# End-of-kernel semaphore waits split between SyncE and GpSimd, and the last attention tile placed ahead of the last half-row matmuls

## The chip, the cores and the metric

The kernel runs on one core of one Trainium2 chip. The metric is device time in microseconds (us) of one execution. A profile of one execution comes with each kernel; its "span" goes from the first to the last recorded instruction and is about 1.7 us shorter than the device time. All times with two or three decimals are from the trace's records or its views. A semaphore is a counter that an instruction can wait for; the end barrier is the last step of the program, in which the engines wait for each other. TensorE is called PE in profile lines (PEld is its weight load), VectorE DVE, ScalarE ACT, GpSimd POOL, SyncE SP; SPq or POOLq is the sequencer of such an engine, which waits for semaphores and issues transfers.

## The reference, cut to what matters

A gate mixes two branches over the same 2048 tokens of width 640:

```python
g = _sigmoid((x * gate_w).sum(-1, keepdims=True))
a = _A_ref(x, A_wqkv, A_wo)          # linear attention, 32 heads of 20
b = _B_ref(x, B_w1, B_w2, B_w3, B_w4)  # token shifts and an MLP with 1728 hidden units
return g * a + (1 - g) * b
# in _B_ref, the end:
h2 = _gelu(_layernorm(x1, axis=-1) @ w3) @ w4
return x1 + h2
```

For the tiles of 128 tokens the kernel computes an attention tile (`a_tile`), keeps it in a buffer, and adds it to the result of the w4 product (`w4_tile`). The hidden width is 1728, which is 13 blocks of 128 rows and one of 64. The 64-row block of four token tiles is done in one go by `w4_half`: two tiles share TensorE's rows, 64 rows each. These are "the half rows" below; the source's word for the step is an excursion.

## The kernel before: the parts that matter

A small scheduler in the source orders the work items of several streams. An item is released by its dependencies; the streams named "AT" (attention tiles) and "W4" meet here:

```python
for t in range(NT):                       # NT = 16
    ...
    IT.add("AT", ("a", t), 1.33, lambda t=t: a_tile(t), deps)
    deps4 = [(("a", t), 0.0), (("w3h", c - c % 2), GEL), (("w3", c, KFF - 1), GEL)]
    if t % 4 == 0:
        deps4.append((("w3", min(c + 1, NCH - 1), KFF - 1), 0.0))
        if t == 0:
            deps4.append((("a", 3), 0.0))
    elif t + 3 < NT:
        deps4.append((("a", t + 3), 0.0))  # attention runs three tiles ahead
    if t % 4 == 0:
        IT.add("W4", ("w4h", t), 0.76, lambda t=t: w4_half(t), deps=deps4)
    IT.add("W4", ("w4", t), 3.5, lambda t=t: w4_tile(t), deps=deps4)
```

PSUM is the memory that TensorE's results go to; the source divides it into eight banks. `w4_half` takes six of them for four tiles; `w4_tile` adds the 13 full-row blocks into them and VectorE evicts each tile with two `scalar_tensor_tensor` instructions (512 and 128 columns), which add the attention tile and write `x_tok`. For tiles 13 to 15 no later attention tile is demanded, so tile 15's attention (called a(15) below) went where the scheduler found it: between w4 tiles 14 and 15.

At the end of the program SyncE waits for every transfer the kernel ever issued:

```python
for want_out in (False, True):
    for k, n in self.dma_cnt.items():
        if k.startswith("out") == want_out:
            self.prog["sp"].append(([("d:" + k, 16 * n)], None, None))
```

There are 35 keys of inputs, weights and on-chip transposes, and 4 of outputs. The last tile's output leaves in two transfers: 512 columns issued by ScalarE (key out1), 128 columns by SyncE (key out2).

## Time and profile before

| | before |
|---|---|
| device time, median of the first three runs | 262.99 us (262.86 to 263.22) |
| span of the profiled run | 261.28 us |
| TensorE busy | 257.5 us, 99% |
| last matmul starts | 258.47 us |
| last eviction ends | 259.08 us |
| last output lands | 260.735 us |
| end | 261.281 us |

First, some lines of the profile page: span, busy time and share of the span by engine with the number of instructions, granted TensorE clock in 40 slices (tenths), and the chain of work that ended last.

```profile
span 261.3 us, 4300 instructions
PE 257.5 (99%) x1699; PEld 135.7 (52%) x1699; DVE 149.1 (57%) x268; ACT 107.0 (41%) x215; POOL 95.7 (37%) x151
PEclk9999999999999999999999999999999999999999
PE 98%; DVE 1%; issue 0%; POOL 0%; POOLq 0%
```

TensorE is the bottleneck, so only two sorts of time can be won by moving work: holes on TensorE, and the tail after its last matmul.

The timeline around the last group of half rows shows one hole. Columns: start, duration in us, engine, line, operation, what is written from what; in brackets the engine's idle time before it and what ended that.

```profile
241.57 1.08 DVE L647 SCALAR_TENSOR_TENSOR x_tok<-ps,stg,abx 128x512 bf16<-128x512 f32 x2 [1.92 <-PE ps L1106]
242.38 0.10 PEld L1088 LDWEIGHTS ps<-w,h2h 64*128 64x128 bf16 x2 [0.29 <-DVE x_tok L647]
242.38 0.39 PE L1088 MATMUL ps<-w,h2h 64*128 64x512 bf16 x2
```

The half rows of tiles 12 to 15 need the bank that VectorE empties for tile 11, and TensorE waits 0.29 us for it. The chain of waits in order of time (start, duration, what) shows the same: an eviction stands in it between two TensorE stretches.

```profile
20.35 0.81 PE ps L787 x6
...
237.37 1.36 PE ps L608 x10
238.73 2.82 PE ps L1106 x13
...
241.57 0.76 DVE x_tok L647
...
242.38 0.39 PE ps L1088 x2
...
243.10 10.70 PE ps L1106 x78
253.80 1.36 PE ps L608 x10
255.16 2.82 PE ps L1106 x13
257.98 0.03 issue
258.00 1.08 DVE x_tok L647 x2
```

The ten matmuls of 1.36 us at 253.80 are a(15). The first line, the first matmuls of a later stage, will serve as a mark. Its time is always taken from this view, which starts the piece about 0.16 us behind the record of its first matmul (20.191 here).

For the tail, the views of two source lines of before give sequencer instructions (columns: how many, duration in ns as minimum/median/maximum, first and last start). The line of the waits, on SyncE after 259 us:

```profile
L316 SPq EVENT_SEMAPHORE  x19: 28/28/28, 259.5 to 260.8; - x19
```

The line that ends the program:

```profile
L296 SPq COMPARE_BRANCH  x1: 41/41/41, 260.9 to 260.9; - x1
```

And of the list of transfers the last two outputs, with their size and the time from issue to landing:

```profile
out_dram<-x_tok ACTq DMA_DIRECT2D x1, 128.0 KB, 1.8
out_dram<-x_tok SPq DMA_DIRECT2D x1, 32.0 KB, 1.6
```

From 259.5 on SyncE works through 19 wait instructions, each holding two semaphores, and the branch holds the 39th. The first 16 stand 0.062 us apart. It looks as if 1.2 us could be removed. But the last transfer is issued at 259.11 and lands at 260.735, and the end of the program can't come before that.

### The profile page before, as it was taken

How to read it: one execution, taken by the hardware profiler on the slowest of the kernel's cores; microseconds unless marked ns; L12 is line 12 of the kernel's file. 1: busy time of each engine (PE TensorE's matmuls, PEld its weight loads, DVE VectorE, ACT ScalarE, POOL GpSimd, SP SyncE). 2: the span in 40 equal slices, each digit the busy share in tenths (PEclk: the TensorE clock that was granted, in tenths of full speed). 3: DMA queues.
4: the chain of work that ended last, by engine and by line, in shares of the span. 5: the costliest groups of instructions: out<-in, count | busy, mean ns of one | idle time of the engine just before them, and what ended most of it. 6: DMA issues, size and time to landing. Idle time of an engine off the chain costs nothing.

```text
span 261.3 us, 4300 instructions
## 1 busy us (share of the span) xinstructions
PE 257.5 (99%) x1699; PEld 135.7 (52%) x1699; DVE 149.1 (57%) x268; ACT 107.0 (41%) x215; POOL 95.7 (37%) x151
## 2 busy tenths in 40 slices
PE   8999999999999999999999999999999999999996
PEld 4555555555555555554444545554455544455553
DVE  1597887899803799979995407992033410143333
ACT  1496677742365757684874240005500045100000
POOL 5003995859774018687654202320011200011000
PEclk9999999999999999999999999999999999999999
DMA  6855999561567795545666600232000020000311
GB/s 200 253 96 139 187 185 151 173 109 24 79 126 103 213 388 166 76 90 67 108 125 126 103 0 0 47 87 69 0 3 0 3 100 0 3 0 0 103 50 50
DMA packets 50691, 24.82 MB, mean 95 GB/s; under 512 B 42052, under 2 KB 49261, under 8 KB 50672
## 3 DMA queue, kind: packets, MB, share of 16 engines
q1 hardware_dynamic: 49280, 21.15, 36.5%
q0 software_dynamic: 1152, 3.28, 5.9%
q8 instruction: 13, 0.21, 0.3%
q10 hardware_dynamic: 240, 0.13, 0.2%
q14 instruction: 6, 0.05, 0.1%
HBM read 12.05 MB, written 2.62 MB: 56 GB/s over the span
## 4 chain that ended last, share of the span: by engine, by line
PE 98%; DVE 1%; issue 0%; POOL 0%; POOLq 0%
PE ps L608 61%; PE ps L1106 21%; PE ps L787 8%; PE ps L860 2%; PE ps L836 1%; PE ps L1020 1%; PE ps L1088 1%; PE ps L619 1%; DVE x_tok L647 1%; PE ps L861 1%; PE ps L934 1%; PE ps L1085 0%; POOL xn L667 0%; POOLq L1249 0%
## 5 line engine op out<-in xcount | busy, mean ns | idle before, releaser
L608 PE MATMUL ps<-xnT,w 128*128 128x512 bf16 x360 | 82.3, 379 | 0.0
L1106 PE MATMUL ps<-w,h2T 128*128 128x512 bf16 (+1 forms) x416 | 58.8, 299 | 0.0
L664 ACT ACTIVATE h2T<-ps 128x512 bf16<-128x512 f32 x52 | 30.4, 600 | 65.7 <-PE ps L608 65.7
L608 PEld LDWEIGHTS ps<-xnT,w 128*128 128x128 bf16 x360 | 34.0, 98 | 36.9 <-issue 0.4
L647 DVE SCALAR_TENSOR_TENSOR x_tok<-ps,stg,abx 128x512 bf16<-128x512 f32 (+1 forms) x32 | 17.2, 551 | 61.6 <-PE ps L1106 61.6
L630 POOL TENSOR_SCALAR abx<-x_tok,stg 128x640 f32<-128x640 bf16 x16 | 15.4, 962 | 100.7 <-DVE x_tok L647 95.1
L1106 PEld LDWEIGHTS ps<-w,h2T 128*128 128x128 bf16 x416 | 32.4, 98 | 25.6 <-issue 1.1
L630 POOL TENSOR_SCALAR xn<-x_tok,st 128x640 bf16<-128x640 bf16 x32 | 33.6, 1055 | 16.6 <-DMA xnT<-xn 16.1
L664 ACT ACTIVATE Er<-ps 128x640 bf16<-128x640 f32 x32 | 22.6, 705 | 18.0 <-PE ps L608 8.5
L663 ACT ACTIVATE junk<-x_tok 128x640 bf16<-128x640 bf16 x32 | 23.6, 737 | 4.8 <-DVE x_tok L645 4.3
L664 ACT ACTIVATE hsT<-ps 128x512 bf16<-128x512 f32 (+1 forms) x32 | 18.9, 594 | 15.1 <-PE ps L608 14.7
L608 PE MATMUL ps<-M_sb,pqnT 128*128 128x512 bf16 (+1 forms) x160 | 24.3, 299 | 0.0
L787 PE MATMUL ps<-pk_tok,x_tok 128*128 128x512 bf16 (+1 forms) x160 | 23.9, 299 | 0.0
L608 PE MATMUL ps<-w,hsT 128*128 128x512 bf16 (+1 forms) x160 | 23.9, 299 | 0.0
L608 PE MATMUL ps<-wkg,xT 128*128 128x512 bf16 (+1 forms) x150 | 22.6, 299 | 0.0
L647 DVE SCALAR_TENSOR_TENSOR abx<-ps,stg,abx 128x640 f32<-128x640 f32 x16 | 14.2, 884 | 14.7 <-PE ps L608 14.7
L608 PEld LDWEIGHTS ps<-w,hsT 128*128 128x128 bf16 x160 | 13.3, 98 | 12.3
L608 PEld LDWEIGHTS ps<-M_sb,pqnT 128*128 128x128 bf16 x160 | 13.1, 98 | 10.4
L608 PE MATMUL ps<-wq,xT 128*128 128x512 bf16 (+1 forms) x120 | 18.3, 299 | 0.0
L630 DVE TENSOR_SCALAR Er<-Er 128x640 bf16<-128x640 bf16 x32 | 11.8, 369 | 9.5 <-ACT Er L664 9.3
L645 DVE SCALAR_TENSOR_TENSOR x_tok<-ps,x_tok 128x640 bf16<-128x640 f32 x16 | 13.1, 821 | 6.9 <-PE ps L608 6.0
L608 PEld LDWEIGHTS ps<-wkg,xT 128*128 128x128 bf16 x150 | 12.2, 97 | 9.0
(71 smaller groups left out, 232.6 us busy)
## 6 DMA issues: line engine op xcount, KB each, us to landing
w<-in_B_w_dram SPq DMA_DIRECT2D x1, 2160.0 KB, 8.4
w<-in_B_w_dram SPq DMA_DIRECT2D x1, 2080.0 KB, 13.8
x_tok<-in_A_x_dram SPq DMA_DIRECT2D x3, 640.0 KB, 5.8
out_dram<-x_tok SPq DMA_DIRECT2D x3, 640.0 KB, 3.5
w<-in_B_w_dram POOLq DMA_DIRECT2D x8, 160.0 KB, 4.7
wq<-in_A_wqkv_dram SPq DMA_DIRECT2D x5, 160.0 KB, 3.9
wkg<-in_A_wqkv_dram SPq DMA_DIRECT2D x5, 160.0 KB, 4.0
wv<-in_A_wqkv_dram POOLq DMA_DIRECT2D x1, 800.0 KB, 7.1
```

The source lines that it names most:

```text
L608: ins = e.matmul(out_ap, l, r, start=(i == 0), stop=(i == n - 1))
L619: ins = e.transpose(o, s_, ident[:])
L630: return engf(lambda e: e.tensor_scalar(out_ap, in_ap, s1, s2, op0, op1), rd, [out_ap], cost=cost)
L645: return dve(lambda e: e.scalar_tensor_tensor(out_ap, in0, scalar, in1, op0, op1, accum_out=accum), rd, [out_ap, accum], cost=cost + 70.0)
L647: return dve(lambda e: e.scalar_tensor_tensor(out_ap, in0, scalar, in1, op0, op1), rd, [out_ap], cost=cost)
L663: return act(lambda e: e.activation(out_ap, in_ap, func, bias=bias, scale=scale, accum_out=accum), rd, wr, cost=cost)
L664: return act(lambda e: e.activation(out_ap, in_ap, func, bias=bias, scale=scale), rd, wr, cost=cost)
L787: ins = e.matmul(o, l, r, start=(t0 + q_ == 0), stop=(t0 + q_ == NT - 1))
L836: ins = e.matmul(ps[:, b, 0:n], xn[:, 0, 0:128], xn[:, 0, 0:128].unsqueeze(1).to_broadcast([128, n // 128, 128]), start=True, stop=True)
L860: e.matmul(ps[:, b, 0:512], l, w[:, k, 0:512], start=(k == 0), stop=(k == KD - 1))
L861: return e.matmul(ps[:, b + 1, 0:n2], l, w[:, k, 512:512 + n2], start=(k == 0), stop=(k == KD - 1))
L1106: ins = e.matmul(o, l, r, start=False, stop=(i == KFF - 1), skip_group_check=(n0 > 0))
```

## The change

The intent: SyncE shall wait for outputs only, with the last transfer last, while GpSimd, which has finished its work, waits for all else; and a(15) shall stand ahead of the last half rows, where TensorE has a hole. The diff, without its two lines that record the order of the transfers:

```diff
-            for want_out in (False, True):
-                for k, n in self.dma_cnt.items():
-                    if k.startswith("out") == want_out:
-                        self.prog["sp"].append(([("d:" + k, 16 * n)], None, None))
+            last = {}
+            for i, k in enumerate(self.dma_order):
+                last[k] = i
+            for k in sorted(last, key=last.get):
+                self.prog["sp" if k.startswith("out") else "pool"].append(([("d:" + k, 16 * self.dma_cnt[k])], None, None))
@@
             if t == 0:
                 deps4.append((("a", 3), 0.0))
+            if t == NT - 4:
+                deps4.append((("a", NT - 1), 0.0))
```

The source's order is not the program's. The build packs two waits into one instruction, takes them in an order of its own, and leaves the first listed wait on the branch. This is what stands on SyncE behind its last transfer in the two built programs (no profile, only the order):

```
before: 16 instructions with inputs (the last: out0, x23), then (out1, x1), (out2, wq0), (out3, x0), branch waits for touch
after:  (out1), (out2, out0), branch waits for out3
```

Here out1 and out2 carry the last two transfers; all other keys were met long before.

## The prediction

> **What bounds the kernel now.** TensorE. The page's first part gives PE 257.5 us busy of a span of 261.3 (99%), the granted clock is full in all slices, and the chain that ended last is 98% PE. Outside PE there is only the tail: the last matmul starts at 258.47, VectorE ends at 259.08, the output transfers issued at 258.79 (ScalarE, 128 KB) and 259.11 (SyncE, 32 KB) land 1.8 and 1.6 us after issue, at about 260.6 and 260.7, and SyncE's branch, drain and the end barrier take the rest to 261.28.
>
> **Part one: the waits.** SyncE's wait instructions stand 0.06 us apart and hold two semaphores each. Before, 19 of them plus the branch stand after SyncE's last transfer, from 259.50 on. That looks like 1.2 us to remove, but it is hidden: the first 16 are through at 260.45, and the next two start at 260.58 and 260.75, held by the two landings, not by their number. The built program takes the waits of one instruction in another order than the source lists them: before, one more wait (an earlier output with an input) and the branch's own (the first load) stand behind the last landing. After the change SyncE keeps two wait instructions and the branch: the ScalarE output, then the last SyncE output with another, then the branch. So one step of 0.06 us goes; the 1 us of input waits goes from under the landing. GpSimd gets 17 waits; its last work ends near 243.5 and it is idle after, so they cost nothing. Expected: 0.06 us.
>
> **Part two: the attention tile.** The TensorE order differs only here: ten matmuls of the last attention tile (1.36 us in the chain) move from behind the third tile of the last w4 group to in front of that group's half-row matmuls; its addition on VectorE moves with it. In the trace these half-row matmuls wait for VectorE (timeline: weight load at 242.38, idle 0.29 before it, released by the x_tok eviction): matmul starts stand 0.34 us apart instead of 0.056. The moved tile has its operands and its bank long before, and covers the eviction. What stays is the step from full rows to half rows: in the three other groups it costs 0.10 us over the normal pitch (starts 0.31 apart instead of 0.21). The Trainium skill, page "TensorEngine Tiling (Array Packing)", section "Key Properties", says that changing the tiling mode drains TensorE; this trace agrees, with about 0.1 us a change. So 0.28 minus 0.10 = 0.19 us. The half rows now wait also for the tail eviction of the tile before (ends 242.65), well inside the 1.36 us. At the end nothing is added: the removed VectorE wait for an output was met at 256.03; the outputs of tiles 12 to 14 leave about 1.2 us later and land by about 257.3, before the last ones start.
>
> **Sum.** 0.19 + 0.06 = 0.25 us of 263: within 2%, smaller than the spread of the three runs before (0.36). I predict 262.74 us, 262.3 to 263.1.
>
> **What would show it.** Right: span near 261.0; no idle time before the last group's half-row load; the last matmul about 0.19 earlier; 0.06 less from the last landing to the end; SyncE with two waits after its last issue. Wrong: a new wait of TensorE near 242 to 244 (bank, or GpSimd's multiply too late), or a landing over 2 us.
>
> **What could make it wrong.** Another bank order delaying an eviction; GpSimd's waits slow enough to reach the barrier; landing times, which vary by a tenth.

## The result, and the profile after

| | before | after |
|---|---|---|
| device time, median of 6 runs each | 263.06 us (262.56 to 263.22) | 262.88 us (262.41 to 263.14) |
| ratio | | 0.9993, 95% interval 0.998 to 1.0006: the same within 2% |
| span of the profiled run | 261.281 us | 261.218 us |
| start of the mark (first matmuls of L787, later L790) | 20.35 us | 20.54 us |
| mark to the start of the last evictions | 237.65 us | 237.46 us |
| last landing to end | 0.546 us | 0.492 us |

A ratio is the mean time of one kernel's fast runs over that of the other's fast runs of the same rounds, so it is not quite the ratio of the medians. All six runs of each were fast.

The difference of the medians is 0.18 us, less than the scatter of one kernel's runs. The profile can tell what the times cannot. The same views, after:

```profile
span 261.2 us, 4301 instructions
PE 257.6 (99%) x1699; PEld 135.9 (52%) x1699; DVE 149.2 (57%) x268; ACT 106.9 (41%) x215; POOL 95.6 (37%) x151
PEclk9999999999999999999999999999999999999999
PE 98%; DVE 0%; issue 0%; POOL 0%; POOLq 0%
```

The timeline at the half rows:

```profile
241.76 1.08 DVE L650 SCALAR_TENSOR_TENSOR x_tok<-ps,stg,abx 128x512 bf16<-128x512 f32 x2 [1.92 <-PE ps L1109]
242.28 1.52 PE L611 MATMUL ps<-M_sb,pqnT 128*128 128x512 bf16 x10
243.73 0.10 PEld L1091 LDWEIGHTS ps<-w,h2h 64*128 64x128 bf16 x2
243.74 0.39 PE L1091 MATMUL ps<-w,h2h 64*128 64x512 bf16 x2
```

a(15) now runs while VectorE evicts tile 11 (until 242.84), and the half rows have no idle time before them. In the records, the start of the half rows follows the matmul before it by 0.151 us; before it was 0.340.

The chain of waits:

```profile
20.54 0.81 PE ps L790 x6
...
237.56 1.36 PE ps L611 x10
238.91 3.53 PE ps L1109 x26
242.45 1.36 PE ps L611 x10
243.81 0.32 PE ps L1091 x2
...
244.46 13.52 PE ps L1109 x91
257.98 0.02 issue
258.00 1.08 DVE x_tok L650 x2
```

The eviction has left the chain. Yet the last evictions start at 258.00 in both profiles: this run entered the mark 0.19 us later and won 0.19 us in the last group. Had one looked only at the end of the chain, the gain would have been missed.

The tail. First the line of the waits, on SyncE after 259 us and on GpSimd after 242 us:

```profile
L319 SPq EVENT_SEMAPHORE  x2: 17/22/28, 260.6 to 260.7; - x2
L319 POOLq EVENT_SEMAPHORE  x17: 42/43/43, 242.9 to 244.3; - x17
```

Then the line that ends the program:

```profile
L298 POOLq DRAIN  x1: 1942/1942/1942, 244.5 to 244.5; - x1
L298 SPq COMPARE_BRANCH  x1: 41/41/41, 260.8 to 260.8; - x1
```

17 of SyncE's 19 wait instructions are gone, but it now just stands still until the landings at 260.558 and 260.726. The two waits and the branch start at 260.575, 260.742 and 260.815, in place of 260.584, 260.752, 260.814 and 260.879: one step less behind the last landing. GpSimd's 17 waits and the one on its branch are over at 244.4 and its drain at 246.5, over 14 us ahead of the barrier at 261.0.

### The profile page after: what moved, and what is told of

Its sections match the earlier page's. It is cut to its first block, busy times and chain, and to the rows that moved or that the text cites. A ratio compares the mean times of both kernels' runs of the same rounds, so it can differ in the third digit from the quotient of the medians.

```text
span 261.2 us, 4301 instructions
## 1 busy us (share of the span) xinstructions
PE 257.6 (99%) x1699; PEld 135.9 (52%) x1699; DVE 149.2 (57%) x268; ACT 106.9 (41%) x215; POOL 95.6 (37%) x151
## 4 chain that ended last, share of the span: by engine, by line
PE 98%; DVE 0%; issue 0%; POOL 0%; POOLq 0%
PE ps L611 61%; PE ps L1109 22%; PE ps L790 8%; PE ps L863 2%; PE ps L839 1%; PE ps L1023 1%; PE ps L1091 1%; PE ps L622 1%; PE ps L864 1%; PE ps L937 1%; DVE x_tok L650 0%; PE ps L1088 0%; POOL xn L670 0%; POOLq L1254 0%
## 5 line engine op out<-in xcount | busy, mean ns | idle before, releaser
L790 PE MATMUL ps<-pk_tok,x_tok 128*128 128x512 bf16 (+1 forms) x160 | 23.9, 299 | 0.0
```

What stands on the lines that cost most here:

```text
L790: ins = e.matmul(o, l, r, start=(t0 + q_ == 0), stop=(t0 + q_ == NT - 1))
```

## The experiments

The theory has two parts. First, the waits on SyncE lay in the shadow of the last landing, and one step of 0.06 us stood behind it. Second, a(15) covers a hole of 0.28 us in front of the half rows, of which 0.10 us comes back as the cost of changing to half rows. The rivals: each removed wait is time saved (then 1 us was lost elsewhere); the hole is the cost of changing rows and not a wait for a bank; the waits only moved their cost to GpSimd. E1 to E4 ran on one chip, E5 to E8 on another; each had its own runs of the kernel before beside it. E5 to E7: only their traces are used. All results were correct.

### E1: the waits alone

Edit, against the changed kernel:

```diff
-            if t == NT - 4:
-                deps4.append((("a", NT - 1), 0.0))
```

> The waits moved, the attention tile left where it was. My theory (the waits lie under the landing of the last outputs, only one wait instruction of 0.06 us stood behind it): two wait instructions on SyncE after its last issue, 0.49 us from the last landing to the end instead of 0.55, the idle time of about 0.29 us before the half-row weight load near 242.4 still there, time 0.06 us under before. Rival (every removed wait instruction is time saved, 17 of 0.06 us each): the span is about 1.0 us shorter, 260.3, and the time near 262.0.

Measured: median 262.91 us of 6 runs, before 263.26 of 11, ratio 0.9998 (0.9982 to 1.0015); one of its runs was at 264.17 with the full clock, which I can't explain and which lifts the mean. The timeline of E1 at the half rows:

```profile
242.30 0.10 PEld L1091 LDWEIGHTS ps<-w,h2h 64*128 64x128 bf16 x2 [0.29 <-DVE x_tok L650]
```

Its waits on SyncE after 259 us:

```profile
L319 SPq EVENT_SEMAPHORE  x2: 17/22/28, 260.5 to 260.7; - x2
```

From last landing to end it took 0.492 us, from mark to last eviction 237.65, as before. So the hole is untouched, and 17 wait instructions fewer on SyncE won 0.054 us. The rival's span of 260.3 did not come (261.15). The size of 0.06 us rests on the trace; the times can't resolve it.

### E2: the tile alone

Edit, against the kernel before: the two lines that E1 takes out, put in.

> The attention tile moved, the waits left on SyncE. My theory (0.28 us of waiting for VectorE's eviction is covered, 0.10 us of changing from full to half rows stays): no idle time before the half-row load, matmul starts there about 0.15 us apart instead of 0.34, last matmul 0.19 us earlier against the one before the group, 19 wait instructions on SyncE and 0.55 us from last landing to end; time 0.19 us under before. Rival (the 0.34 us are the change of row mode, not the eviction): the starts stay about 0.34 us apart and the time is that of before.

Measured: median 262.84 us of 6 runs, ratio 0.9998 (0.9976 to 1.002), again with one outlier (264.62). The timeline of E2 at the half rows:

```profile
243.70 0.10 PEld L1088 LDWEIGHTS ps<-w,h2h 64*128 64x128 bf16 x2
```

Its waits on SyncE after 259 us:

```profile
L316 SPq EVENT_SEMAPHORE  x19: 28/28/28, 259.5 to 260.8; - x19
```

No idle time before the half rows; their start follows the matmul before by 0.152 us; from mark to last eviction 237.47, 0.18 less than before; from landing to end 0.549, as before. The hole was the wait for the bank. The two parts add up: E1's tail and E2's stretch are those of the changed kernel. The times do not show this: the medians of E1 and E2 lie 0.35 and 0.42 us under before's, more than the traces give (0.05 and 0.18), and each with an outlier. Nothing is read from times at this size.

### E3: last output listed first

Edit, against the changed kernel:

```diff
-            for k in sorted(last, key=last.get):
+            for k in sorted(last, key=last.get, reverse=True):
```

> The changed kernel with its waits listed in the opposite order, last output first, since the built program puts the first listed wait on the branch itself. Theory: the branch then waits for the last landing directly and no wait instruction stands behind it; 0.42 us from last landing to end (0.49 in the changed kernel, 0.55 before); time 0.07 us under the changed kernel. Rival (order plays no part, or the branch costs more when it has to wait itself): 0.49 us or more.

Measured: 0.423 us from last landing to end; the branch starts 0.017 us behind the landing (0.089 in the changed kernel). SyncE's waits are both taken up at 259.5, and the second one stands until ScalarE's output lands:

```profile
L319 SPq EVENT_SEMAPHORE  x2: 17/524/1032, 259.5 to 259.5; - x2
```

The branch of E3, in the view of the line that ends the program:

```profile
L298 SPq COMPARE_BRANCH  x1: 41/41/41, 260.7 to 260.7; - x1
```

Median 262.63 us of 5 runs, ratio to before 0.9981 (0.9969 to 0.9993). By the traces this version beats both kernels, the changed one by 0.07 us and before by 0.31 (0.19 + 0.05 + 0.07); it was not timed beside the changed kernel. The timed gain against before is larger than that sum but its interval holds it. So the intent "last one last" was met in the source and not in the program; listing it first does it.

### E4: three times the input waits on SyncE

Edit, against the kernel before:

```diff
-            for want_out in (False, True):
+            for want_out in (False, False, False, True):
```

> The kernel before, each input wait listed three times: 54 wait instructions on SyncE instead of 19. Theory (the waits are hidden until they reach the landing, with about 0.15 us of room): 259.50 plus 54 steps of 0.062 is 262.85, so the end comes at about 263.3, 2.0 us later than before, and the landing no longer sets the end. Rival one (waits that are already met cost next to nothing, at any number): the time of before. Rival two (each costs in full): 35 times 0.062, 2.2 us later.

Measured: span 263.301; from the mark (20.47) to the end 242.83 us, 1.90 more than before's 240.93 (the other 0.12 us of the longer span are a later start); median 265.20 us of 4 runs, ratio 1.0098 (1.0067 to 1.0129, one run at 267.06 with a clock of 0.996). The last output had landed at 260.848 and the end came 2.45 us later. The waits of E4 on SyncE, and then its branch:

```profile
L316 SPq EVENT_SEMAPHORE  x54: 28/28/28, 259.6 to 262.8; - x54
```

```profile
L296 SPq COMPARE_BRANCH  x1: 41/41/41, 262.9 to 262.9; - x1
```

A met wait costs 0.062 us of SyncE's time, but this reaches the clock on the wall only once the queue of waits outlasts the landing. Before, they had about 0.2 us of room: the 18th instruction, which holds the last output, could have started at 259.499 + 17 x 0.0617 = 260.55 and started, on the landing, at 260.752. Thirty-five more at 0.0617 are 2.16 us; less the room, 1.96. (E4's own steps are a little shorter, 0.0608, which gives 1.91.) "Each costs in full" and "next to nothing" both fall, the first by 0.26 us only.

### E5: the tile behind the half rows

Edit, against the changed kernel:

```diff
-            if t == NT - 4:
-                deps4.append((("a", NT - 1), 0.0))
         elif t + 3 < NT:
             deps4.append((("a", t + 3), 0.0))
+        elif t == NT - 3:
+            deps4.append((("a", NT - 1), 0.0))
```

> The waits as changed; the attention tile as early as one tile of the last group after the half rows, so earlier than before, but behind them instead of ahead. Theory (only what stands in front of the half rows can cover the eviction): idle time of 0.29 us and matmul starts of 0.34 us are back, and from the first attention tile's first matmul to the last matmul it takes the same as with the waits alone, 0.19 us more than the changed kernel. Rival (an early attention tile helps by itself, for instance by taking its addition off VectorE's end): the 0.19 us stay gained.

Measured, one look (262.82 us): the hole is back, and mark to last eviction took 237.65 us, as in before and E1. The timeline of E5 at the half rows:

```profile
242.25 0.10 PEld L1091 LDWEIGHTS ps<-w,h2h 64*128 64x128 bf16 x2 [0.29 <-DVE x_tok L650]
```

Being early is worth nothing; only the place in front of the half rows is.

### E6 and E7: eight and sixteen times the waits on GpSimd

Edit, against the changed kernel (8, then 16):

```diff
+                for rep in range(1 if k.startswith("out") else 8):
-                self.prog["sp" if ...
+                    self.prog["sp" if ...
```

> The changed kernel with each input wait listed eight times on GpSimd, some 140 wait instructions. In the changed kernel's trace they stand 0.087 us apart there (0.062 on SyncE) from 243.0 on. Theory: they end near 255.2, over 5 us ahead of the end barrier at 261.0, so the span stays that of the changed kernel, 261.0 to 261.3, and 0.49 us from last landing to end. Rival (polling of semaphores on another engine disturbs SyncE or TensorE): a span longer by more than 0.3 us or a slower step between matmuls.

> The same with sixteen, some 280 wait instructions. Theory: they end near 267.4, past the barrier, and GpSimd now sets the end: span about 267.9, 6.7 us longer. Rival (GpSimd's waits are free at any number): 261.2.

The waits on GpSimd, in E6:

```profile
L320 POOLq EVENT_SEMAPHORE  x140: 17/43/43, 242.7 to 255.0; - x140
```

E6: 140 wait instructions over at 255.0, span 261.015, 0.492 us from landing to end, mark to last eviction 237.47: no cost. E7: span 269.875 us, 8.66 over the changed kernel's 261.218 and not the 6.7 that I expected. The line that ends the program, in E7:

```profile
L298 POOLq COMPARE_BRANCH  x1: 43/43/43, 267.5 to 267.5; - x1
L298 POOLq DRAIN  x1: 1945/1945/1945, 267.7 to 267.7; - x1
```

The waits end at 267.5, near the 267.4 expected (they stand 0.089 us apart and start at 242.7), but I had left out GpSimd's drain, which takes 1.94 us behind them although it had nothing left to do. It could have been foreseen: the changed kernel's trace has it at the same length (1942 ns at 244.5, above), and in before it ends 1.97 us behind GpSimd's last multiply. With the tile move undone (E1) GpSimd's waits ran from 254.2 to 255.6 and its drain to 257.7, still 3 us ahead of the barrier.

### E8: no input waits at all

Edit, against the changed kernel:

```diff
-                self.prog["sp" if k.startswith("out") else "pool"].append(...)
+                if k.startswith("out"):
+                    self.prog["sp"].append(...)
```

> The changed kernel with no input waits at the end at all (every consumer has waited for its input itself; the outputs are still waited for). Theory: moving them to GpSimd had already made them free, so nothing more is gained: 0.49 us from last landing to end, time within 0.1 us of the changed kernel. Rival (GpSimd's waits still cost at the barrier): up to 1.3 us less (15 of 0.087 us).

Measured: median 262.85 us of 6 runs, before 263.21 of 11, ratio 0.9979 (0.9953 to 1.0005; before has a run of 265.19 in it); 0.492 us from landing to end, mark to last eviction 237.46, mark to end 240.69 against the changed kernel's 240.68. Nothing is gained over the changed kernel, whose median beside its own runs of before was 262.88. The waits on GpSimd are free where they stand.

## Why the prediction was right, point by point

- **Predicted 262.74 us (262.3 to 263.1), measured 262.88.** The result lies in the range, and "within 2%" came true. That proves little: the range also holds the 262.99 us of the kernel before, so no gain at all would have passed, and the interval of the ratio, 0.998 to 1.0006, holds 1. What bears the prediction out are the stretches below.
- **The waits: 0.06 us, measured 0.054.** The reading that 1 us of waits lay under the landing was right: E1 won no more, and E4 showed where the shadow ends, at 1.90 us for 35 added instructions against 2.0 expected (the room under the landing was 0.20 us and not 0.15).
- **The tile: 0.28 minus 0.10, 0.19 us; measured 0.340 to 0.151 us between starts, 0.189.** E2 and E5 show the bank wait as the cause. The part that stayed, 0.151 instead of the usual 0.056, is a step of 0.095 us from full to half rows; it is the same on the way back (0.148 instead of 0.053). The Trainium skill, page "TensorEngine Tiling (Array Packing)", section "Key Properties", says that a change of tiling mode drains TensorE; the traces show extra time at the change, which fits. That draining is the mechanism no run here tests. A rival fits as well: at both changes the weight load (0.093 to 0.096 us) starts only 0.004 us before its matmul, while a load between full rows starts 0.054 us ahead; a load that is no longer hidden would cost about the same.
- **No new wait on TensorE, no delay at the end: right.** The tail eviction of tile 11 ended at 242.84 (242.65 foreseen), the output of tile 14 landed at 257.35 (257.3 foreseen).
- **The sum: 0.25 us.** From mark to end of span it is 261.281 - 20.35 = 240.93 before and 261.218 - 20.54 = 240.68 after, 0.25 us less.
- **"The last matmul about 0.19 earlier", "span near 261.0": not so in that profile.** It started at 258.469 against 258.472, and the span was 261.22. I compared times since the start of two executions and took the start as fixed. It isn't: the mark lies between 20.22 and 20.54 us in the ten profiles. From mark to last eviction they fall into two groups without overlap: 237.65 (before, E1, E4, E5) and 237.46 to 237.47 (after, E2, E3, E6, E7, E8). The sign to look for should have been a stretch and not a moment.
- **"The granted clock is full in all slices" was the page's line and hid the start.** In before's records the short matmuls (128 columns) stand 0.107 us apart until 6.5 us and 0.056 after. The change came between 4.1 and 7.1 us in the ten profiles. The Trainium skill, page "TensorE: Matmul & The Clock Gate", Part 1 ("The HAM clock gate"), says that the window deciding this runs freely and so the start of full speed varies from run to run, by 0.5 us either way. These traces agree that it varies, but by more, and they show no window: full speed had come by 5.1 us in E4 and not before 7.0 us in the changed kernel, 1.9 us later. The first matmuls here also wait for their inputs, so the activity before the change is not the same in each. Waits for the first input transfers differ as well (E4 waited 0.36 us for x_tok at 6.34). How much of the 0.32 us each makes was not separated.

What stays open: the single runs of 264 us and more, in before as well as in the variants, of which there is no profile; GpSimd's drain, of which only the length is known; and whether the 0.095 us of a change of rows is draining or a weight load.

## What to carry to other kernels

Count a list of waits at the end against the landing that it ends with: in this kernel, what was shorter than the landing was worth nothing, and what counted was only the instructions behind the last landing, in the order of the built program and not of the source. When TensorE stands before a group that needs a bank just being emptied, look for independent matmuls with a bank of their own that come later anyway, and put them in front; the same work put behind won nothing. And effects under the scatter of the times can be measured to about 0.01 us from a mark behind the noisy start to a mark behind the change, if several variants agree on it.

## What the Trainium skill lacked or had wrong

- "TensorEngine Tiling (Array Packing)" says that a mode change drains TensorE but not what it costs: 0.095 us going from 128 rows to 64 (starts 0.151 apart instead of 0.056), and 0.148 instead of 0.053 on the way back.
- No page gives the cost of a wait instruction that is already met: starts 0.062 us apart on SyncE and 0.087 to 0.089 on GpSimd, two semaphores each. The nearest, "Advanced Engine Details and Errata", section "Network/Comms", has 50 to 100 ns for reading a semaphore's value from a sequencer, of the same size.
- No page says which of several waits listed for one instruction the build leaves on the instruction itself (here the first), nor in what order it takes the others; it is worth 0.07 us at the end of the program (E3).
- No page gives a length like that of GpSimd's drain at the end of this program: 1.94 us with nothing left to do (E7, where it lay on the path).
- "DMA: Bandwidth & Descriptors", section "Anatomy of one DMA — SWDGE (gpsimd) path", puts the fixed cost of a transfer at about 2.0 us for that path and gives no such sum for transfers issued from SyncE or ScalarE; the outputs here, issued from these two, landed 1.6 us (32 KB) and 1.8 us (128 KB) after issue.
- "TensorE: Matmul & The Clock Gate", Part 1, has the start of full speed vary by 0.5 us either way from run to run; in the ten profiles here it varied by at least 1.9 us, with waits for inputs among the first matmuls.
